# A scheduled order, later weight loads, two-bank PSUM tiles and 256-token MLP chunks in an attention, Fourier-mixing and MLP kernel

## Chip, cores and metric

One core of one Trainium2 chip. The time is device microseconds of one execution; a lower time is better. The sessions ran on different chips; in three of them the kernel before had medians of 359.4 to 360.1 us. So where two medians of different sessions lie close, the ratios, each to the kernel before on the same chip, are the safer measure.

## The reference, cut to what matters

```python
# attention: B=4 batches, H=8 heads, S=768 tokens, D=64; 8 global keys, 96 local keys
scores = scale * (q @ k^T) + bias          # bias by distance; masked outside the band
a = softmax(scores);  attn = a @ v         # -> x of shape (B, S, 512)
# mixing and MLP
X = fft(fft(x, axis=1), axis=2);  u = x + real(X)
un = (u - mean(u)) / sqrt(var(u) + 1e-6)
out = u + maximum(un @ w_ch1, 0) @ w_ch2   # 512 -> 2048 -> 512
```

Everything is float32 outside; the kernel computes its matmuls in float16 with float32 accumulation.

## The kernel before

Each batch passes through attention, mixing (the Fourier transform, as folds on DVE and matmuls `py` and `pu`), normalisation, and the MLP (`ph` is the first matmul, `pg` the second). Rows are handled by residue modulo 6, so a row tile is 128 rows with one residue. Python code emits all instructions in one order, guided by a rough clock (`ck`). Each engine then runs its own part of that order, in order; below, DVE's u adds stand behind a multiply that waits 3.27 us. The kernel uses PSUM, the memory that matmuls write, as eight banks of 512 float32 per partition. DVE and ACT read a finished bank out (an *eviction*), which makes it free for the next matmuls.

```python
XB = 5
BUFS = {"x": XB, "ph": 2, "pg": 1}               # 8 banks, each a tile of its own
def bank(tag, name, dtype=FP32):
    n = 512 if dtype == FP32 else 1024
    return ps.tile([P, n], dtype, tag=tag, name=name, bufs=BUFS[tag])
...
def u_u(b, rs):                                   # one row tile of the mixing's last matmul
        pu = bank("x", f"pu_{b}_{rs}")
        for rd, (r2, d2, mir) in enumerate(src):
            o = pu[:, rd * P:(rd + 1) * P]        # contiguous: one column class after the other
            for c in range(2):
                nc.tensor.matmul(o, yy[:, c, :], t2_sb[:, rd, ...], start=(c == 0), stop=(c == 1))
        VT(u.rearrange("p (n r) -> p r n", r=4), pu.rearrange("p (r n) -> p r n", r=4),
           XR[b][:, rs, :].rearrange("p (n r) -> p r n", r=4), op=ALU.add)
...
def u_ph(c, jb):                                  # MLP chunk of 384 tokens: three row tiles
        ph = bank("ph", f"ph_{c}_{jb}")
        for d in range(ND):
            nc.tensor.matmul(ph[:, 0:CH], w1[:, d, jb * P:(jb + 1) * P], UNT[(b, half)][:, d, :], ...)
...
def load_w():                                     # all weights on the GpSimd queue
    for a in range(4):
        nc.gpsimd.dma_start(w1[:, :, a * 512:(a + 1) * 512], ...)
    for a in range(4):
        nc.gpsimd.dma_start(w2[:, 4 * a:4 * a + 4, :], ...)
...
            if which == "A":                      # attention and mixing: one fixed list
                A[ia][3]()
                ia += 1
                if not wload and ia == 12:
                    load_w()
```

The softmax here doesn't subtract the row's maximum and nothing guards it: scores larger than these inputs give would overflow.

Of the kernel before, what the change touches and what calls it, by code (L numbers as in the profile page):

```python
# [17 lines left out]
class Clock:  # L18


    SEM = 0.12

    def __init__(self):
        self.t = {"PE": 0.0, "ACT": 0.0, "DVE": 0.0, "POOL": 0.0}
        self.tok = {}
        self.ring = {}

    def at(self, needs):
        return max([self.tok[n] for n in needs], default=0.0)
# [4 lines left out]
    def adv(self, eng, cost, after=0.0):  # L34
        end = max(self.t[eng], after + self.SEM) + cost
        self.t[eng] = end
        return end

    def slot(self, tag, bufs):
        r = self.ring.setdefault(tag, [0.0] * bufs)  # L40
        return r.pop(0)

    def give(self, tag, when):
        self.ring[tag].append(when)
        self.ring[tag].sort()

    def slot_at(self, tag, bufs, n=1):
        r = self.ring.setdefault(tag, [0.0] * bufs)
        return r[n - 1] if len(r) >= n else 1e9


def mm_us(n, k=1):
    return k * max(n / 2400.0 + 0.0025, 0.029)


@with_exitstack
def kernel(
# [20 lines left out]
    CH = S // 2  # L78
# [9 lines left out]
    dist = np.zeros((P, 512))  # L88
    dist[:, 0:256] = np.where(band, rel, np.where(kk < NG, NL, far))
    dist[:, 256:512] = np.where(band, rel, far)  # L90
    pp = np.arange(P)[:, None]
# [17 lines left out]
    gb = np.zeros((32, 2))  # L109
    for half in range(2):  # L110
        for h in range(4):
            gb[h * NG:(h + 1) * NG, half] = -slopes[4 * half + h] * NL
# [12 lines left out]
    XB = 5  # L125
    UB = 7
    BUFS = {"x": XB, "ph": 2, "pg": 1}
    ck = Clock()

    def bank(tag, name, dtype=FP32):  # L130
        n = 512 if dtype == FP32 else 1024
        return ps.tile([P, n], dtype, tag=tag, name=name, bufs=BUFS[tag])

# [3 lines left out]
    dist_sb = kon.tile([P, 512], FP16, tag="dist", name="dist")  # L137
    gb_sb = kon.tile([32, 2], FP32, tag="gb", name="gb")
# [5 lines left out]
    mhalf = kon.tile([P, NS], FP32, tag="mhalf", name="mhalf")  # L144
# [3 lines left out]
    vG = [kon.tile([32, 2, 4, 66], FP16, tag=f"vG{i}", name=f"vG{i}") for i in range(2)]  # L148


    def flex(cost_act, cost_dve, after, on_act, on_dve):

        ea = max(ck.t["ACT"], after + ck.SEM) + cost_act
        ed = max(ck.t["DVE"], after + ck.SEM) + cost_dve
        if ea <= ed:
            on_act()
            return ck.adv("ACT", cost_act, after)
        on_dve()
        return ck.adv("DVE", cost_dve, after)

    stage = {}

    def load(b, hp):
        for nm, src in (("q", q), ("k", k), ("v", v)):
            if b == 0 and nm != "v":
                if hp == 0:
                    stage[(nm, "all")] = wk.tile([P, HP, S], FP32, tag="hT", name=f"{nm}s0", bufs=2)
                t = stage[(nm, "all")][:, hp, :]
            elif b == 0 and hp >= 2:
                t = wk.tile([P, S], FP32, tag="unT", name=f"{nm}s_{b}_{hp}", bufs=2)  # L170
            else:
                t = wk.tile([P, S], FP32, tag=f"{nm}s", name=f"{nm}s_{b}_{hp}", bufs=2 if nm == "v" else 1)
            stage[(nm, b, hp)] = t
            for s in range(2):
                dst = t.rearrange("p (i h d) -> p i h d", h=2, d=Dh)[:, :, s, :]
                nc.sync.dma_start(dst, src[b, 2 * hp + s].rearrange("(i p) d -> p i d", p=P))  # L176
            base = 3.5 + 2.3 * hp if b == 0 else max(ck.t["PE"], ck.tok.get(("cast", nm, b, hp - 1), 0)) + 6
            ck.tok[("ld", nm, b, hp)] = base + {"q": -0.7, "k": 0.0, "v": 0.7}[nm]

    T16 = {}  # L180
    TT = {}

    def u_cast(b, hp, nm):
        def run():
            src = stage[(nm, b, hp)]
            after = ck.tok[("ld", nm, b, hp)]
            if nm == "v":
                dst = v16[b % 2][:, :, 2 * hp:2 * hp + 2, 0:Dh]
                src = src.rearrange("p (i h d) -> p i h d", h=2, d=Dh)
                if b == 0:  # L190
                    nc.gpsimd.tensor_copy(dst, src)  # L191
                    end = ck.adv("POOL", 1.0, after)
                else:
                    nc.gpsimd.tensor_copy(dst, src)
                    end = ck.adv("POOL", 1.0, after)
            else:
                t = wk.tile([P, S], FP16, tag=f"{nm}16", name=f"{nm}16_{b}_{hp}", bufs=2)
                T16[(nm, b, hp)] = t
                end = flex(0.83, 0.5, after,
                           lambda: nc.scalar.activation(t, src, AF.Copy),  # L200
                           lambda: nc.vector.tensor_copy(t, src))  # L201
            ck.tok[("cast", nm, b, hp)] = end
            nxt = HP * b + hp + 1
            if nm == "v" and HP <= nxt < HP * B:
                load(*divmod(nxt, HP))
        return ([("ld", nm, b, hp)], None, 0, run)

    def u_trans(b, hp, nm):
        def run():
            src = T16.pop((nm, b, hp))  # L210
            pt = bank("x", f"pt{nm}_{b}_{hp}", FP16)
            dst = wk.tile([P, S], FP16, tag=f"{nm}T", name=f"{nm}T_{b}_{hp}", bufs=3)
            TT[(nm, b, hp)] = dst
            free = ck.slot("x", XB)
            for i in range(NS):
                nc.tensor.transpose(pt[:, i * P:(i + 1) * P], src[:, i * P:(i + 1) * P], idn)
            e = ck.adv("PE", mm_us(P, NS), max(ck.at([("cast", nm, b, hp)]), free)) + 0.15
            end = flex(0.85, 0.55, e,
                       lambda: nc.scalar.activation(dst, pt[:, 0:S], AF.Copy),
                       lambda: nc.vector.tensor_copy(dst, pt[:, 0:S]))  # L220
            ck.give("x", end)
            ck.tok[(nm + "T", b, hp)] = end
            if nm == "k":
                for s in range(2):
                    c0 = 16 * (hp % 2) + 8 * s
                    nc.gpsimd.tensor_copy(kG[b % 2][64 * s:64 * s + 64, hp, c0:c0 + NG],
                                          dst[64 * s:64 * s + 64, 0:NG])
                    ck.tok[("kG", b, hp)] = ck.adv("POOL", 0.15, end)
        return ([("cast", nm, b, hp)], "x", 1, run)

    def u_score(b, hp, g):
        def run():
            qT, kT = TT[("q", b, hp)], TT[("k", b, hp)]
            n1 = 224 if g < 2 else P
            n = 256 + n1
            pa = [bank("x", f"sc_{b}_{hp}_{g}_{s}") for s in range(2)]
            free = max(ck.slot("x", XB), ck.slot("x", XB))
            for i, c0, w in ((2 * g, 0, 256), (2 * g + 1, 256, n1)):
                for s in range(2):
                    lo = 64 * s  # L240
                    nc.tensor.matmul(pa[s][:, c0:c0 + w], kT[lo:lo + 64, i * P:(i + 1) * P],  # L241
                                     qT[lo:lo + 64, i * P:i * P + w], start=True, stop=True)
            e = ck.adv("PE", 0.25, max(ck.at([("qT", b, hp), ("kT", b, hp)]), free)) + 0.15
            er = wk.tile([P, 2, 480], FP16, tag="er", name=f"er_{b}_{hp}_{g}", bufs=2)
            for s in range(2):
                nc.scalar.activation(er[:, s, 0:n], pa[s][:, 0:n], AF.Exp, 0.0, 0.125)  # L246
                end = ck.adv("ACT", 0.19 + n / 1200, e)
                ck.give("x", end)
            m0 = 0 if g == 0 else 256
            nc.vector.tensor_tensor(expst[hp][:, :, g * 512:g * 512 + n], er[:, :, 0:n],  # L250
                                    mk[:, 2 * hp:2 * hp + 2, m0:m0 + n], op=ALU.mult)
            ck.tok[("ex", b, hp, g)] = ck.adv("DVE", 0.15 + n / 960, end)
        return ([("qT", b, hp), ("kT", b, hp)], "x", 2, run)

    def u_vg(b):
        def run():
            pv = bank("x", f"pvg_{b}")
            free = ck.slot("x", XB)
            for half in range(2):
                for h in range(4):  # L260
                    c0 = half * 256 + h * 64
                    nc.tensor.matmul(pv[0:32, c0:c0 + 64], sel_sb[0:NG, h * 32:(h + 1) * 32],  # L262
                                     v16[b % 2][0:NG, 0, 4 * half + h, 0:Dh], start=True, stop=True)
# [155 lines left out]
    def u_y(b, n):  # L419
        needs = [("w", b)]  # L420

        def run():
# [24 lines left out]
            if n == len(YP) - 1:  # L447
                mirror(b, end)
# [326 lines left out]
```

## Time and profile before

| | before |
|---|---|
| time, median of 4 runs | 361.1 us (359.4 to 361.5) |
| span of the profiled run | 357.4 us |
| busy PE, DVE, ACT, POOL | 272.4, 210.5, 142.6, 51.5 us |
| last v of batch 0 cast at | 46.3 us |
| first ph at | 87.0 us |
| after the first ph: length, PE busy, PE idle | 270.4, 238.7, 31.6 us |

PE is TensorE, PEld its weight loads, DVE VectorE, ACT ScalarE, POOL GpSimd and SP SyncE. L569 is a source line; lines move by a few between kernels, so the same group has a number near it in the others. Busy time by stretches, cut at the first ph. Its columns are the stretch and its length, then busy us (and instructions) of PE, weight loads, DVE, ACT and POOL, then the mean granted clock of PE, the DMA share and GB/s. The kernel before:

```profile
0.00:87.02 87.02, 33.69 (x293) 21.97 (x294) 45.12 (x114) 25.21 (x46) 19.74 (x42) 0.96 0.79 146
87.02:357.40 270.38, 238.74 (x1808) 133.54 (x1807) 165.37 (x357) 117.43 (x236) 31.74 (x71) 0.96 0.38 90
```

The idle time of a stretch is its length less PE's busy time: 53.3 us before the first ph and 31.6 after.

### The profile page before, as it was taken

What the parts mean: (1) busy time and instruction counts of PE and PEld (TensorE: products, weight loads), DVE (VectorE), ACT (ScalarE), POOL (GpSimd) and SP (SyncE); (2) the same over time, 40 slices, a digit from 0 to 9 for tenths busy, and PEclk for the clock granted to TensorE, in tenths of its full rate; (3) what the DMA queues carried; (4) which work ended last, traced back from release to release, by engine and by line L of the source; (5) the groups of instructions that cost most, each with busy time, mean ns of one, the idle gap of its engine ahead of it and who ended that gap; (6) DMA issues with size and microseconds to landing.
All of it is one profiled execution on the core that took longest, in us unless ns stands there. A gap on an engine that the chain in (4) does not pass through costs nothing.

```text
span 357.4 us, 5463 instructions
## 1 busy us (share of the span) xinstructions
PE 272.4 (76%) x2100; PEld 155.5 (44%) x2100; DVE 210.5 (59%) x470; ACT 142.6 (40%) x282; POOL 51.5 (14%) x113
## 2 busy tenths in 40 slices
PE   0540079246899998838999989389999994799995
PEld 0320045134555554635555546255545452555542
DVE  0730049978555689796456976984567778810011
ACT  1840053012587730215778312056965220355310
POOL 1760010031121000312120003121110003100000
PEclk9999999996999999969999999879999998799999
DMA  9999990400397606101986043009900250000011
GB/s 187 217 201 196 196 244 1 172 6 1 88 207 166 132 2 193 73 29 43 213 175 132 31 124 142 29 2 202 192 33 32 88 179 0 31 0 29 31 58 60
DMA packets 87306, 36.99 MB, mean 104 GB/s; under 512 B 76016, under 2 KB 83440, under 8 KB 87280
## 3 DMA queue, kind: packets, MB, share of 16 engines
q1 hardware_dynamic: 83056, 32.45, 40.5%
q0 software_dynamic: 4224, 4.19, 6.9%
q8 instruction: 16, 0.26, 0.3%
q14 instruction: 10, 0.08, 0.1%
HBM read 31.39 MB, written 9.44 MB: 114 GB/s over the span
## 4 chain that ended last, share of the span: by engine, by line
PE 57%; DVE 22%; SPq 8%; DMA 7%; issue 2%; POOL 2%; ACT 1%; POOLq 0%; DVEq 0%
PE pg L598 21%; PE ph L569 19%; DMA vs<-in_v_dram 7%; SPq L176 7%; DVE u L495 7%; DVE st L503 5%; PE pav L324 4%; PE sc L241 3%; DVE ob L603 2%; PE py L429 2%; DVE un L523 2%; PE ptu L545 2%; PE pav L313 2%; PE pu L490 2%; PE py L432 1%
## 5 line engine op out<-in xcount | busy, mean ns | idle before, releaser
L569 PE MATMUL ph<-unT,w 128*128 128x384 f16 x512 | 97.9, 329 | 2.7 <-ACT unT L549 2.7
L598 PE MATMUL pg<-w,hT 128*128 128x512 f16 x384 | 94.3, 379 | 3.3 <-DVE ob L603 2.6
L574 ACT ACTIVATE hT<-ph 128x384 f16<-128x384 f32 x117 | 57.7, 499 | 60.5 <-PE ph L569 60.2
L569 PEld LDWEIGHTS <-w 128*128 128x128 f16 x512 | 48.2, 99 | 42.2 <-issue 10.0
L250 DVE TENSOR_TENSOR ex<-er,mk 128x960 f16<-128x960 f16 (+1 forms) x48 | 31.8, 665 | 40.4 <-ACT er L246 40.2
L598 PEld LDWEIGHTS <-hT 128*128 128x128 f16 x384 | 36.2, 98 | 40.6 <-issue 6.0
L246 ACT ACTIVATE er<-sc 128x480 f16<-128x480 f32 (+1 forms) x96 | 45.9, 556 | 8.1 <-PE sc L241 6.4
L603 DVE TENSOR_TENSOR ob<-pg,u 128x512 f32<-128x512 f32 x24 | 16.5, 688 | 40.3 <-PE pg L598 38.6
L545 PE MATMUL ptu<-ident,un 128*128 128x128 f16 x96 | 12.2, 266 | 28.6 <-DVE un L523 28.1
L495 DVE TENSOR_TENSOR u<-pu,xr 128x512 f32<-128x512 f32 x24 | 25.4, 1057 | 8.4 <-PE pu L490 8.4
L549 ACT ACTIVATE unT<-ptu 128x512 f16<-128x512 f16 x12 | 7.2, 597 | 55.8 <-PE ptu L545 55.8
L441 ACT ACTIVATE y<-py 128x512 f16<-128x512 f32 x16 | 9.2, 596 | 40.2 <-PE py L432 39.9
L545 PEld LDWEIGHTS <-un 128*128 128x128 f16 x96 | 7.9, 121 | 33.1 <-DVE un L523 33.1
L332 DVE TENSOR_TENSOR x<-pav,rc 128x256 f16<-128x256 f32 x48 | 20.4, 425 | 1.6
L241 PE MATMUL sc<-qT,kT 64*128 64x256 f16 x192 | 19.0, 290 | 2.9 <-ACT q L200 2.1
L324 PE MATMUL pav<-v,ex 128*128 128x65 f16 x352 | 20.6, 207 | 0.0
L262 PE MATMUL pvg<-v,ident 8*32 8x64 f16 x32 | 2.3, 198 | 23.2 <-POOL v L191 23.0
L324 PEld LDWEIGHTS <-ex 128*128 128x128 f16 x352 | 15.2, 105 | 8.2 <-issue 4.4
L503 DVE BATCH_NORM_STATS2 st<-u 128x6 f32<-128x512 f32 x24 | 16.7, 695 | 0.8
L523 DVE TENSOR_SCALAR un<-u,mv,rstd 128x512 f16<-128x512 f32 x24 | 13.1, 599 | 5.3 <-POOL rstd L509 5.3
L455 POOL COPY rev<-y 128x2 f16<-128x2 f16 x4 | 0.8, 192 | 99.0 <-PE py L432 99.0
L201 DVE CAST k<-ks 128x768 f16<-128x768 f32 x13 | 7.2, 556 | 12.9 <-DMA ks<-in_k_dram 12.9
(81 smaller groups left out, 309.4 us busy)
## 6 DMA issues: line engine op xcount, KB each, us to landing
qs<-in_q_dram SPq DMA_DIRECT2D x32, 192.0 KB, 3.7
ks<-in_k_dram SPq DMA_DIRECT2D x32, 192.0 KB, 4.0
vs<-in_v_dram SPq DMA_DIRECT2D x32, 192.0 KB, 4.5
out_dram<-ob SPq DMA_DIRECT2D x24, 256.0 KB, 2.0
w<-in_moe_w_ch_dram POOLq DMA_DIRECT2D x8, 512.0 KB, 15.6
xd<-x SPq DMA_DIRECT2D x4, 768.0 KB, 3.7
xr<-xd SPq DMA_DIRECT2D x4, 768.0 KB, 4.9
t<-t1m SPq DMA_DIRECT2D x1, 384.0 KB, 16.7
```

What stands on the lines that cost most here:

```text
L176: nc.sync.dma_start(dst, src[b, 2 * hp + s].rearrange("(i p) d -> p i d", p=P))
L241: nc.tensor.matmul(pa[s][:, c0:c0 + w], kT[lo:lo + 64, i * P:(i + 1) * P], qT[lo:lo + 64, i * P:i * P + w], start=True, stop=True)
L246: nc.scalar.activation(er[:, s, 0:n], pa[s][:, 0:n], AF.Exp, 0.0, 0.125)
L250: nc.vector.tensor_tensor(expst[hp][:, :, g * 512:g * 512 + n], er[:, :, 0:n], mk[:, 2 * hp:2 * hp + 2, m0:m0 + n], op=ALU.mult)
L324: nc.tensor.matmul(o, lhsT, v16[b % 2][:, i, h, 0:65], start=(j < 2 and a == 0), stop=(a == len(ops) - 1), skip_group_check=True)
L495: VT(u.rearrange("p (n r) -> p r n", r=4), pu.rearrange("p (r n) -> p r n", r=4), XR[b][:, rs, :].rearrange("p (n r) -> p r n", r=4), op=A ...
L503: nc.vector.bn_stats(st, u)
L545: nc.tensor.transpose(pt[:, c * P:(c + 1) * P], un[:, c * P:(c + 1) * P], idn)
L569: nc.tensor.matmul(ph[:, 0:CH], w1[:, d, jb * P:(jb + 1) * P], UNT[(b, half)][:, d, :], start=(d == 0), stop=(d == ND - 1))
L574: lambda: nc.scalar.activation(dst, ph[:, 0:CH], AF.Relu),
L598: nc.tensor.matmul(pg, HT[c][:, jb, t * P:(t + 1) * P], w2[:, jb, :], start=(jb == 0), stop=(jb == NJ - 1))
L603: nc.vector.tensor_tensor(ob, pg, UT[(b, rs)], op=ALU.add)
```

## The change

A list scheduler with a clock per engine, a queue of loads and priorities (mixing, then attention, then pg, then ph) decides the order of all work. Attention and mixing get two-bank PSUM tiles, so that one eviction serves two banks. MLP chunks shrink from three row tiles to two, so that an MLP can start earlier. The weight loads also move: w1 after the third v cast, w2 to batch 0's mixing. The core of the diff, of some 1,500 lines:

```diff
-    BUFS = {"x": XB, "ph": 2, "pg": 1}
+    RING = {"xx": 2, "ph": 2, "pg": 2}
+    cd = [ps.tile([P, 2, 512], FP32, tag=f"c{i}", name=f"c{i}", bufs=1) for i in range(2)]
...
     def bank(tag, name, dtype=FP32):
-        n = 512 if dtype == FP32 else 1024
-        return ps.tile([P, n], dtype, tag=tag, name=name, bufs=BUFS[tag])
+        if tag in "CD":                                  # batch 0's attention borrows both
+            return cd["CD".index(tag)]
+        if tag in turn:                                  # ph and pg: slices of one tile each
+            turn[tag] += 1
+            return cd["ph pg".index(tag) // 3][:, turn[tag] % 2, :]
+        return ps.tile([P, 2, 512 if dtype == FP32 else 1024], dtype, tag=tag, name=name, bufs=RING[tag])
...
-                o = pu[:, rd * P:(rd + 1) * P]
+                o = pu[:, a, :].rearrange("p (n r) -> p r n", r=4)[:, rd, :]
...
-            VT(u.rearrange("p (n r) -> p r n", r=4), pu.rearrange("p (r n) -> p r n", r=4),
-               XR[b][:, rs, :].rearrange("p (n r) -> p r n", r=4), op=ALU.add)
+                VT(u, pu, XR[b][:, r0:r1 + 1:r1 - r0, :], op=ALU.add)
...
-                if not wload and ia == 12:
-                    load_w()
+        for i in range(8):
+            needs = [("v", 0, 2)] if i == 0 else [("rv", 0, 0)] if i == 4 else [("wl", i - 1)]
+            pl.later([("POOL", 0.85, lambda i=i: wload(i))], needs, ...)
...
+        pl.run([(MIX, True), (ATT, True), (PG, False), (PH, False)])
```

## The prediction

> **What bounds the kernel now.** I read the busy shares of the slices first, then busy time stage by stage, then the wait list, and last the timeline of the first 90 us. TensorE (PE) is the busiest engine, 272.4 of 357.4 us, and the slices show where it is not:
>
> ```profile
> PE   0540079246899998838999989389999994799995
> ...
> DMA  9999990400397606101986043009900250000011
> ```
>
> One digit is 8.9 us. PE is at 9 through most of the second half, but nearly empty in the first five slices while the DMA is full, and it dips (8 3 8, 9 3 8, 4 7) once per batch. I cut the span by stage:
>
> ```profile
> 0.00:25.00 25.00, 9.59 (x72) 5.86 (x73) 10.52 (x30) 13.86 (x25) 14.34 (x30) 1.00 1.20 202
> 25.00:46.00 21.00, 0.00 (x0) 0.00 (x0) 1.12 (x2) 0.00 (x0) 0.00 (x0) 1.00 1.22 199
> 46.00:64.20 18.20, 14.68 (x136) 8.19 (x135) 13.39 (x41) 7.76 (x15) 1.19 (x3) 1.00 0.47 102
> 64.20:87.00 22.80, 9.41 (x84) 7.92 (x85) 20.06 (x41) 3.58 (x6) 4.20 (x9) 0.85 0.20 70
> 87.00:313.60 226.60, 199.45 (x1601) 113.43 (x1601) 160.81 (x350) 103.47 (x208) 31.74 (x71) 0.95 0.43 100
> 313.60:357.40 43.80, 39.30 (x209) 20.11 (x206) 4.58 (x7) 13.96 (x29) 0.00 (x0) 0.98 0.10 36
> ```
>
> Columns: stretch and length, then busy us of PE, weight loads, DVE, ACT, POOL, then granted clock, DMA share, GB/s. From 25 to 46 us no engine computes and the DMA moves 199 GB/s. At 64.2 batch 0's attention is complete; up to 87.0, where the first MLP matmul (ph) starts, batch 0's mixing runs on DVE (20.06 of 22.8 us) with PE mostly empty. From 87.0 on it is a PE-bound kernel: 238.75 us busy in 270.4, so 31.6 idle. The waits name the culprits:
>
> ```profile
> PE ptu L545 <- DVE un L523: 28.1, 8, 6.9
> ...
> POOL v L191 <- DMA vs<-in_v_dram: 22.0, 1, 22.0
> ...
> PE pg L598 <- DVE ob L603: 2.6, 3, 1.1
> ```
>
> The first is the per-batch dip: in the mixing PE waits up to 6.9 us for a normalised tile. About 21 of its 28.1 us lie after 87.0. The second is the hole at the start, and the timeline shows its cause:
>
> ```profile
> 20.95 9.72 SPq L176 DMA_DIRECT2D vs<-in_v_dram  x2
> ...
> 46.29 0.82 POOL L191 CAST v<-vs 128x768 f16<-128x768 f32 x1 [22.04 <-DMA vs<-in_v_dram]
> ```
>
> The last head pair's v is issued at 20.95 and usable only at 46.29, because all eight weight loads (4.19 MB as written) were queued from 16.3 us on and share the DMA with it; and the fixed order puts a step that needs every v ahead of scores and outputs that do not.
>
> [...] from 20 to 46 us the input queue got about 1.6 MB of 5.4. [...]
>
> ```profile
> 103.16 0.65 PE ph L569 x4
> ...
> 139.34 3.61 PE pg L598 x16
> ```
>
> 0.65/4 = 162 ns for 384 columns; 3.61/16 = 226 ns for 512 columns, with the last drain in it. [...] The residual add of 512 took 688 ns [...], but the strided u add 1057:
>
> ```profile
> L495 DVE TENSOR_TENSOR u<-pu,xr 128x512 f32<-128x512 f32 x24 | 25.4, 1057 | 8.4 <-PE pu L490 8.4
> ```
>
> [...] the change makes the pu output stride 4.
>
> **The change part by part.**
>
> *Start.* Only half the weights (w1, 2.1 MB) may start early, after the third v is cast; w2 waits for mixing and batch 1's loads for batch 0's round trip. The nine transfer pairs through the third v are 3.5 MB plus constants; at some 205 GB/s they land near 20 us, so w1 starts near 21. About 1.1 MB of input is then left, and w1 takes 2.1/0.134 = 16 us at the share weights had before ((5.4-1.6) MB in 26 us, about 140). I put the last v at 37 us, not 46. The new order has by then done all other scores, so cast, outputs and norm need about 5 us, not 18: attention of batch 0 ends near 42 instead of 64.2.
>
> *Mixing to first ph.* Fold of the second half 3.2, first fold_d part 1.9, second 2.1, py with its eviction 2.7, pu 1.0, [...] statistics 2 x 0.69 + 2 x 0.18 = 1.75, four small POOL steps 1.4, two normalisations on ACT 1.3, transposes 0.8, eviction 1.0, semaphores about 1: 19 us against 22.8, because it waits for one pair of row tiles instead of three. First ph near 61-62: 25 us earlier.
>
> *PE work after that.* ph goes from 512 x 384 to 768 x 256 columns: 512 x 162 = 83.0 us against 768 x 109 = 83.8. Matmul columns are otherwise equal (2100 instructions become 2360, the 256 ph and four tiny ones). So 239 us of busy time stay, perhaps 3 less from fewer cold stretches (clock 0.85 in the mixing stage).
>
> *DVE and ACT.* u adds 12 x 1.22 = 14.6 instead of 25.4; half as many reciprocals, -4; norms 24 x 0.69 = 16.5 instead of 20.4; 17 of 24 normalisations move to ACT, -9; transposed q/k copies all come to DVE, +4; folds in one piece, -5. DVE about 192 instead of 210, ACT about 137 instead of 143. Neither bounds before or after; this only shortens the dip.
>
> *Dips.* The order keeps earlier MLP chunks for the gaps. For batch 1 that fails: all three chunks of batch 0 are done before its mixing matmuls, and only the next batch's scores fill in. DVE chain there about 22 us, PE work in it 19, plus latency: 5-6 us lost. Batches 2 and 3 have ph and pg between: 1-2 each. So 21 becomes 8, gain 13.
>
> *What it adds.* I also read which instruction each wait in the built program names. The two ph banks are now slices of one tile, and so are the two pg banks, and waits are by tile: a ph unit waits for the eviction of the unit before it, in the other bank; two ph units in a row are evicted only when both are done. The ring of two is a ring of one. Working through the 53 such ph waits (eviction plus signalling 0.9 us for one, 1.4 for two, less the matmuls placed between) leaves 14 us, the 21 pg waits (0.69 add + 0.2) 8 us. The same sum for the kernel before gives 3 + 4, where the wait list shows about 5. So +15 us.
>
> *Sum.* After the first ph: 239 - 3 + (31.6 - 13 + 15) = 270, as long as before (270.4). The gain is the start's 25: 61.5 + 270 = 331 span; runs lie 3.4 above the profiled span (360.8 against 357.4), giving 335. My whole-tile sum counts each wait in full, though other waits and drain overlap (ph lasts 326 ns but is spaced 162) will swallow a third: -5. **330 us.**
>
> **Rivals.** *A: the strided pu output costs PE.* 192 matmuls; if each doubles from 56 to 107 ns, +10 us, a third of it in the dips. [...] Against: each has its own weight load of about 98 ns, which may hide it. Makes it 335-340. *B: the start stays load-bound*, since w1 alone still competes with the last v: if it lands at 44 instead of 37, 337. *C: the whole-tile waits are mostly hidden or the dips vanish entirely*: 315. *D: DVE becomes the bound*: 192 us in 330 is 58%, so no; only if its order is wrong in a mixing stage. *E: in-order stalls where the scheduler's clock and the chip disagree* (single q/k staging buffer, POOL casts behind late loads): 10-15 us, 345. *F: the early start is a mirage because the PE sum bounds*: no, 239 + 61 is well below.
>
> **Range and chances.** A, B and E each raise it by 5-15 and are partly exclusive; C lowers it by 15. So 330, 8 in 10 within 309 to 345. "Same" needs over 353.6, two of the bad rivals at full size: 4%; slower needs the plan to fail: 2%.
>
> **What would show it.** In the changed profile: last v of batch 0 cast at 34-40 us and first ph at 58-66; busy PE 230-242 after it; the u add near 1.22 us; pu per matmul near 60 ns (A wrong) or above 100 (A right); many PE waits of ph on hT evictions, 10-20 us in sum where there were none; one dip near mixing 1, next to none at 2 and 3. The prediction is wrong if the first ph comes as late as 75, or if these ph waits are under 5 us, or if a wait on a load appears after batch 0.

One term of the sum: the add of 1024 columns, 1.22 us, in the list from mixing to the first ph. With it the list came to 19.4 us, without it 18.15. The forecast used 19: first ph at 42 + 19 = 61 to 62; then 61.5 + 270 = 331 of span, + 3.4 for the time, - 5 for waits swallowed: 330 us. The term can also be had from the profile before, as an estimate: DVE's TENSOR_TENSOR took 425 ns for 256 columns (x<-pav,rc) and 688 for 512 (ob<-pg,u), so 688 + 2 x 263 = 1.21 us for 1024; in the changed kernel it took 1.218. For the doubling that rival A supposes no reason is left; 56 and 107 ns are in the profile before, but as the pu spacing at granted clocks of 1.00 and 0.50.

- 109 ns for 256 columns: the ph spacing in the changed kernel.
- 0.69 us: 695 ns of a BATCH_NORM_STATS2 and 688 of a TENSOR_TENSOR of 512 columns in the kernel before.
- 1.6 MB of 5.4: a misreading, 1.12 of 5.17 by the DMA packets.
- The "last drain": pg matmuls of the kernel before start 216 ns apart and are drawn 379 long; 15 x 216 + 379 = 3.61 us.
- "Semaphores" and "signalling": in the timeline of the changed kernel below, ACT ends at 288.37 + 1.09 = 289.46 and the ph that needs both evictions starts at 289.51. From 288.17, when the ph unit before has made way for pg, it is 0.85 us to the pg that waits for one eviction (289.02) and 1.34 to that ph, where the forecast has 0.9 and 1.4.
- 3 us less for "cold" stretches, those of a low granted clock: a guess; after the first ph the clock was 0.96 before and 0.98 after.

## The result, and the profile after

The changed kernel takes **341.2 us** (median of 4, 339.8 to 341.4) against 361.1: ratio 0.945, 95% interval 0.941 to 0.949. A ratio here is the mean time of one kernel's runs over that of the other's of the same rounds, so it is not quite the ratio of the medians.

The slices of the changed kernel; one digit is 8.5 us:

```profile
PE   0596385898989986589998999898998999989894
```

The two empty slices near the start are gone, but there are many 8s where the second half had 9s before. Busy time by stretches says the same with numbers (cut where batch 0's attention is complete and at the first ph):

```profile
0.00:37.96 37.96, 22.56 (x212) 14.69 (x212) 23.56 (x57) 20.85 (x27) 9.26 (x25) 1.00 1.12 215
37.96:60.00 22.04, 11.74 (x81) 9.07 (x82) 16.99 (x37) 4.88 (x8) 8.69 (x19) 0.98 0.98 189
60.00:339.70 279.70, 249.62 (x2068) 162.30 (x2067) 141.13 (x241) 101.77 (x151) 61.82 (x121) 0.98 0.35 89
```

The first ph starts 27 us earlier (60.0 against 87.0), yet what follows takes 279.7 us instead of 270.4: 9.3 us are given back. The timeline of the changed kernel (start, duration, engine, line, what; in brackets the idle time before and who ended it) shows the start as it was meant, and one thing that was not:

```profile
24.21 0.74 POOL L913 DMA_DIRECT2D w<-in_moe_w_ch_dram  x1
29.12 0.82 POOL L343 CAST v<-u 128x768 f16<-128x768 f32 x1 [4.17 <-DMA u<-in_v_dram]
...
132.00 1.91 PE L723 MATMUL pu<-t,zy 128*128 128x128 f16 x16 [0.69 <-ACT zy L659]
```

The last v is cast at 29.1 instead of 46.3. The pu matmuls, in a stretch at granted clock 1.00, take 1.91 us for 16; their starts lie 109 ns apart (the last is drawn 314 ns long). The kernel before had 22 in 1.39 us at that clock, about 55 ns apart. But 64 of its 192 pu matmuls ran at a granted clock of 0.50, and lay 107 ns apart there. In the groups of the changed kernel (columns: in the prediction) the u add has become one contiguous add of 1024:

```profile
L740 DVE TENSOR_TENSOR u<-pu,xr 128x1024 f32<-128x1024 f32 x12 | 14.5, 1218 | 7.3 <-PE pu L723 6.5 <-DMA vs<-in_v_dram 0.9
```

The wait list (who waited for whom: us in total, times, longest) has lost the prediction's wait of ptu for un, and has these instead; `c` is the tile of both ph banks at L814 and of both pg banks at L837:

```profile
PE c L837 <- DVE ob L848: 7.1, 11, 0.8
...
PE c L837 <- ACT hT L820: 5.1, 20, 0.3
PE c L814 <- ACT hT L820: 4.0, 9, 0.7
```

They sum to 16.2 us (ACT and DVE write hT, the evicted ph; DVE adds pg into ob). The timeline of the last stage, where nothing but MLP is left, shows one period of them (PE's matmuls, and ACT's evictions up to the second wait):

```profile
286.43 1.91 PE L814 MATMUL c<-unT,w 128*128 128x256 f16 x16
288.17 0.59 PE L837 MATMUL c<-w,hT 128*128 128x512 f16 x2
288.37 1.09 ACT L820 ACTIVATE hT<-c 128x512 f16<-128x512 f32 x2 [5.67 <-PE c L814]
289.02 0.60 PE L837 MATMUL c<-w,hT 128*128 128x512 f16 x2 [0.26 <-ACT hT L820]
289.51 1.91 PE L814 MATMUL c<-unT,w 128*128 128x256 f16 x16
```

Two ph units and one part of pg take 289.51 - 286.43 = 3.08 us, of which the profile calls 0.26 idle.

### The profile page after: what moved, and what is told of

Its sections match the earlier page's. It is cut to its first block, busy times and chain, and to the rows that moved or that the text cites. A ratio compares the mean times of both kernels' runs of the same rounds, so it can differ in the third digit from the quotient of the medians.

```text
span 339.7 us, 5828 instructions
## 1 busy us (share of the span) xinstructions
PE 283.9 (84%) x2360; PEld 186.1 (55%) x2360; DVE 181.7 (53%) x332; ACT 127.5 (38%) x185; POOL 79.8 (23%) x165
## 4 chain that ended last, share of the span: by engine, by line
PE 64%; ACT 8%; DVE 7%; SPq 7%; DMA 5%; POOL 4%; issue 4%; POOLq 0%; DVEq 0%; ACTq 0%
PE c L814 26%; PE c L837 22%; ACT hT L820 5%; SPq L320 4%; PE pav L494 3%; PE pu L723 3%; PE sc L397 2%; DMA u<-in_v_dram 2%; DVE ob L848 2%; PE pav L481 2%; SPq L309 2%; PE pt L369 2%; DMA vs<-in_v_dram 2%; PE py L643 2%; DMA xr<-xd 1%
## 5 line engine op out<-in xcount | busy, mean ns | idle before, releaser
L837 PE MATMUL c<-w,hT 128*128 128x512 f16 x384 | 98.9, 380 | 12.6 <-DVE ob L848 7.1
L814 PE MATMUL c<-unT,w 128*128 128x256 f16 x768 | 98.6, 279 | 5.1 <-ACT hT L820 4.0
L820 ACT ACTIVATE hT<-c 128x512 f16<-128x512 f32 x85 | 48.0, 596 | 120.7 <-PE c L814 113.1
L814 PEld LDWEIGHTS <-w 128*128 128x128 f16 x768 | 75.4, 100 | 26.3 <-issue 11.6
L837 PEld LDWEIGHTS <-hT 128*128 128x128 f16 x384 | 33.3, 97 | 53.5 <-ACT hT L820 15.9
L405 ACT ACTIVATE er<-sc 128x960 f16<-128x960 f32 (+1 forms) x42 | 38.0, 910 | 31.6 <-PE sc L397 30.8
L848 DVE TENSOR_TENSOR ob<-c,u 128x512 f32<-128x512 f32 x24 | 16.5, 689 | 55.1 <-PE c L837 55.0
L410 DVE TENSOR_TENSOR ex<-er,mk 128x960 f16<-128x960 f16 (+1 forms) x48 | 33.4, 700 | 21.3 <-ACT er L405 21.1
L333 POOL CAST qk<-qs 128x768 f16<-128x768 f32 x24 | 21.2, 903 | 36.5 <-PE pt L369 21.5
L692 POOL COPY ww<-zy 128x512 f16<-128x512 f16 x16 | 9.4, 613 | 61.5 <-PE py L643 43.1
L375 DVE COPY qkT<-pt 128x1536 f16<-128x1536 f16 x16 | 15.3, 954 | 13.1 <-PE pt L369 13.1
L369 PE MATMUL pt<-ident,qk 128*128 128x128 f16 x192 | 15.8, 242 | 4.5 <-DVE qk L331 2.4
L659 ACT ACTIVATE zy<-py 128x512 f16<-128x512 f32 (+1 forms) x12 | 9.6, 810 | 23.4 <-PE py L646 17.9
L768 ACT ACTIVATE un<-u,rstd 128x512 f16<-128x512 f32 x17 | 13.4, 810 | 12.3 <-POOL rstd L758 11.1
L397 PE MATMUL sc<-qkT 64*128 64x256 f16 (+2 forms) x168 | 16.0, 281 | 1.0 <-DVE unT L796 1.0
```

The source lines that it names most:

```text
L333: nc.gpsimd.tensor_copy(d, s)
L369: nc.tensor.transpose(pt[:, w, j * P:(j + 1) * P], src[:, w, j].rearrange("p h d -> p (h d)"), idn)
L375: V.tensor_copy(TT[n], pt[:, :, 0:S])
L397: nc.tensor.matmul(pa[:, s, c0:c0 + cw], TT[n][lo:lo + 64, 1, i * P:(i + 1) * P], TT[n][lo:lo + 64, 0, i * P:i * P + cw], start=True, stop ...
L405: A(er[0][:, :, 0:w], pa[:, :, 0:w], AF.Exp, 0.0, 0.125)
L410: VT(expst[hp][:, :, g * 512:g * 512 + w], er[0][:, :, 0:w], mk[:, 2 * hp:2 * hp + 2, m0:m0 + w], op=ALU.mult)
```

## The experiments

Twelve kernels ran, three timed rounds each, all with correct results. The orders of instructions called equal below are so in the traces. Ratios are against runs of the kernel before on the same chip (359.4 to 360.1 us median). First ph and the length after it are from each profiled run.

| kernel | time, us | ratio (95%) | first ph | after it |
|---|---|---|---|---|
| before | 361.1 | 1 | 87.0 | 270.4 |
| changed | 341.2 | 0.945 (0.941-0.949) | 60.0 | 279.7 |
| b_latew: before, weights late | 340.4 | 0.945 (0.942-0.949) | 67.7 | 271.5 |
| a_earlyw: changed, weights early | 361.0 | 1.002 (0.997-1.007) | 80.4 | 279.9 |
| a_sep: changed, ph and pg banks apart | 317.9 | 0.882 (0.878-0.886) | 59.7 | 257.2 |
| a_sep_ph: changed, ph banks alone apart | 324.8 | 0.904 (0.900-0.907) | 60.0 | 263.8 |
| b_slice: b_latew, ph banks as slices | 382.8 | 1.064 (1.061-1.067) | 67.5 | 313.5 |
| a_pu: changed, pu contiguous | 337.9 | 0.938 (0.934-0.942) | 59.5 | 276.7 |
| a_pu_sep: a_sep and a_pu together | 316.0 | 0.877 (0.872-0.882) | 60.8 | 254.3 |
| a_perm_sep: a_sep, u in class order | 314.8 | 0.873 (0.868-0.878) | 59.4 | 250.6 |
| a_q: changed, round trip off the SP queue | 342.0 | 0.949 (0.946-0.953) | 60.6 | 280.9 |
| a_pu_sep_q: all three | 316.8 | 0.880 (0.877-0.884) | 61.4 | 253.8 |
| a_sep_prio: a_sep, MLP first | 366.5 | 1.018 (1.014-1.023) | 59.5 | 303.6 |
| a_sep_look1: a_sep, look-ahead 1 | 329.1 | 0.915 (0.911-0.918) | 62.9 | 264.3 |

The theory was the prediction's: a gain at the start, from the weights no longer competing with inputs and from the order; and a loss after it, from waits by whole tile. The rivals were that the strided pu output is the loss, that an in-order stall is, or that the order alone makes the gain.

### Are the weights the gain? (b_latew, a_earlyw)

In the kernel before, with the same order on PE, ACT and DVE:

```diff
-                if not wload and ia == 12:
-                    load_w()
-                    wload = True
+                if ia == 16:          # after batch 0's third v cast
+                    load_w1()
+                if ia == NA0 + 9:     # as batch 0's mixing starts
+                    load_w2()
```

> The kernel before, with its old order and tiles; only the weight loads move: the four of w1 are queued after batch 0's third v is cast, the four of w2 where batch 0's mixing starts. Theory (the hole at the start is weights competing with the last inputs): last v of batch 0 cast at 29 to 36 us instead of 46.3, first ph 10 to 15 us earlier than 87.0, time 346 to 352 us against 361, so over half of the change's gain at the start comes from this alone. Rival (the fixed order is what holds the start, or the weights are now late for ph): first ph still after 83 us, time within 3 us of 361.

And the reverse, in the changed kernel, whose scheduler then places some later work differently too:

```diff
-            needs = [("v", 0, 2)] if i == 0 else [("rv", 0, 0)] if i == 4 else [("wl", i - 1)]
+            needs = [("v", 0, 1)] if i == 0 else [("wl", i - 1)]
```

> The changed kernel with its own order, but all eight weight loads queued early again, from batch 0's second v cast on, as in the kernel before. Theory (weights compete with inputs): last v of batch 0 cast at 42 to 48 us instead of 29.1, first ph at 70 to 75 instead of 60.0, time 350 to 356 against 341. Rival (the scheduled order hides late inputs): first ph before 64, time within 4 us of 341.

Moving eight loads in the old kernel gave **340.4 us**, as fast as the whole change, and better than expected. Putting them back in the changed kernel gave **361.0**, as slow as the kernel before, 5 us worse than expected. b_latew, timeline and busy time by stretches:

```profile
26.68 0.82 POOL L191 CAST v<-vs 128x768 f16<-128x768 f32 x1 [2.23 <-DMA vs<-in_v_dram]
```

```profile
67.70:339.20 271.50, 239.09 (x1808) 133.71 (x1807) 165.18 (x357) 117.33 (x236) 31.66 (x71) 0.96 0.39 92
```

a_earlyw, the same two views:

```profile
48.52 0.82 POOL L343 CAST v<-u 128x768 f16<-128x768 f32 x1 [23.85 <-DMA u<-in_v_dram]
```

```profile
80.40:360.30 279.90, 250.39 (x2068) 162.91 (x2067) 137.76 (x237) 101.58 (x152) 60.06 (x120) 0.97 0.34 85
```

The last v comes at 26.7 to 29.1 us with w1 alone behind it and at 46.3 to 48.5 with all eight loads; the first ph follows, and the length after it does not move (271.5 against 270.4; 279.9 against 279.7). So 87.0 - 67.7 = 19.3 of the 27.0 us gained at the start are the weights, and 67.7 - 60.0 = 7.7 the new order with its smaller chunks. Taken the other way round, with a_earlyw, they are 80.4 - 60.0 = 20.4 and 6.6. The early loads are not only more: they are also issued at 15.5 to 16.3 us, against 20.5 to 21.1, and no run separates their number from their time. The net gain of the change is no more than the weights; all else came out at about zero. Either the rest is worth nothing, or it is worth much and something takes it away.

### Do waits by whole tile take it away? (a_sep, a_sep_ph, b_slice)

Four single-bank tiles take the place of the two double ones, in the same four banks, once batch 0's attention has given those up. Every engine has the same instructions in the same order; only waits differ.

```diff
-    cd = [ps.tile([P, 2, 512], FP32, tag=f"c{i}", name=f"c{i}", bufs=1) for i in range(2)]
+    cdp = tc.tile_pool(name="cdp", bufs=1, space=bass.MemoryType.PSUM)
+    cdt = cdp.__enter__()
+    cd = [cdt.tile([P, 2, 512], FP32, tag=f"c{i}", name=f"c{i}", bufs=1) for i in range(2)]
+    mlp = {}
...
-            turn[tag] += 1
-            return cd["ph pg".index(tag) // 3][:, turn[tag] % 2, :]
+            if not mlp:
+                cdp.__exit__(None, None, None)
+                mlp[0] = ctx.enter_context(tc.tile_pool(name="mlp", bufs=1, space=bass.MemoryType.PSUM))
+            return mlp[0].tile([P, 512], FP32, tag=tag, name=name, bufs=2)
```

> The changed kernel with the two ph banks and the two pg banks as four tiles of their own, opened when batch 0's attention has given up the two double banks; engine orders identical, only waits differ. Theory of the prediction (waits by whole tile cost 22 us in sum, a third hidden): time 326 to 334 against 341, ph pairs in the last stage spaced about 2.7 us instead of 3.08. Rival C (these waits are mostly hidden): over 337.

**317.9 us: 23.3 less** (22.7 by the ratios), more than expected. The stage after the first ph falls from 279.7 to 257.2 us. The same place in the timeline of a_sep (PE's matmuls and the first of ACT's evictions), and its stretch after the first ph:

```profile
285.49 1.91 PE L819 MATMUL ph<-unT,w 128*128 128x256 f16 x16
286.56 0.60 ACT L825 ACTIVATE hT<-ph 128x512 f16<-128x512 f32 x1 [4.59 <-PE ph L819]
287.23 1.03 PE L842 MATMUL pg<-w,hT 128*128 128x512 f16 x4
288.10 1.91 PE L819 MATMUL ph<-unT,w 128*128 128x256 f16 x16
```

```profile
59.70:316.90 257.20, 243.93 (x2068) 164.59 (x2067) 140.09 (x241) 104.34 (x151) 64.14 (x121) 0.97 0.39 96
```

The period is 288.10 - 285.49 = 2.61 us, against 3.08, without a gap. The profile had called only 0.26 of these 0.47 us idle. The same shows in the sum: of the 22.5 us saved after the first ph, idle time gives 30.1 - 13.3 = 16.8, and **busy PE gives 249.6 - 243.9 = 5.7**, though the work is the same. The reason, as a reading of the trace: pg matmuls start 216 ns apart but are drawn 379 ns long, so the last one before a wait covers its first 0.16 us. The changed kernel has 32 gaps right after a ph or pg matmul and a_sep has 2, which makes (32 - 2) x 0.16 = 4.8 of the 5.7 us, as an estimate. So a sum of PE's waits reads low.

a_sep_ph leaves the pg banks as slices of one tile:

```diff
+            if tag == "ph":
+                return mlp[0].tile([P, 512], FP32, tag=tag, name=name, bufs=2)
+            turn[tag] += 1
+            return mlp["pg"][:, turn[tag] % 2, :]      # one double tile, as in the change
```

> The changed kernel with only the two ph banks as tiles of their own; the two pg banks stay slices of one tile. Splits the 23 us. By the prediction's sums (14 us of ph waits, 8 of pg waits) ph alone should give about 15 of the 23: 325 to 328 against 341. Rival (one of them is nearly all, since a ph wait also delays the pg behind it): below 321 if it is all ph, above 333 if pg.

324.8 us: ph's share is 16.4 us and pg's 6.9 by the medians, 15 and 8 by the ratios. The prediction's sums were 14 and 8. The ph share is not visible as waits of ph alone (4.0 us in the list). Where two ph units follow each other, both are evicted only when both are done: in the timeline above ACT writes hT first at 288.37, after the second unit, and in a_sep at 286.56, during it. So it is the pg part that reads the first one's hT that waits. The wait list of a_sep_ph agrees: PE's 5.1 and 4.0 us of waits for hT shrink to 0.5, and the 7.1 for ob stay (7.2).

The opposite test puts this one thing into the old order (b_latew):

```diff
+    phs = ps.tile([P, 2, 512], FP32, tag="phs", name="phs", bufs=1)
     def bank(tag, name, dtype=FP32):
+        if tag == "ph":
+            turn[0] += 1
+            return phs[:, turn[0] % 2, :]
```

> The kernel before with late weights, and one thing taken from the change: its two ph banks become the two halves of one tile. Order of all work unchanged. Theory (waits go by tile, so a ring of two slices is a ring of one): the same sum that gave 14 us of ph waits for the changed kernel gives about 54 us more here (121 waits, up to 0.9 us each, since this order puts more ph units back to back): 375 to 395 against 340.4. Rival (the cost seen in the changed kernel is peculiar to its order, not to slices): under 350.

382.8 against 340.4, so **42.4 us slower**, within the expected range. Its wait list names the line, again with fewer us than are lost:

```profile
PE phs L575 <- ACT hT L580: 30.0, 44, 1.4
```

So the cost belongs to the slices, not to the new order. Why the new order suffers less is not tested. By count of the traces fewer of its ph units follow another directly, 32 of 96 against 49 of 128.

### What does the strided pu output cost? (a_pu, a_pu_sep, a_perm_sep)

```diff
-                o = pu[:, a, :].rearrange("p (n r) -> p r n", r=4)[:, rd, :]
+                o = pu[:, a, rd * P:(rd + 1) * P]
...
-                VT(u, pu, XR[b][:, r0:r1 + 1:r1 - r0, :], op=ALU.add)
+                for a, r in enumerate((r0, r1)):
+                    VT(u[:, a].rearrange("p (n r) -> p r n", r=4), pu[:, a].rearrange("p (r n) -> p r n", r=4),
+                       XR[b][:, r, :].rearrange("p (n r) -> p r n", r=4), op=ALU.add)
```

> The changed kernel with the pu output contiguous again (each of the four column classes in its own 128 columns), and the u add done as two strided adds of 512, as in the kernel before; order of all other instructions the same. Theory (stride-4 PSUM writes slow the matmul): pu spaced 55 ns instead of 109, busy PE 10 us less; the adds cost 2 x 1.06 instead of 1.22 us per pair; about two thirds of the 10 us is saved, time 333 to 337 against 341. Rival (the pu time lies in dips and the slower adds eat it): within 2 us of 341.

337.9 us, 3.3 less (2.6 by the ratios, whose intervals just overlap); expected were 4 to 8. At granted clock 1.00 the spacing is 55 ns again, and the adds take 2 x 1.08 us. PE is busy 277.4 us instead of 283.9: 6.5 less, not the 10 expected.

> The changed kernel with both edits: ph and pg banks as four tiles, and the pu output contiguous with two strided adds. With the banks apart PE is busy nearly without a gap after 60 us but for batch 1's mixing, so a saving in PE now counts in full. Theory (strided pu costs 10 us of PE, of which the three later batches' 7.7 us lie on the bounded path): 309 to 312 against 317.9 with the banks alone, busy PE about 268. Rival (the slower adds or something else fills the place, as the 3.3 us of the pu edit alone suggest): 314 to 318.

316.0 us against 317.9: 1.9 less (ratios 0.877 and 0.882, with overlapping intervals). The theory was wrong twice: PE's work fell by 6.8 us (278.3 to 271.5), not 10, and the time by less. Two stretches show it, the first with batch 1's mixing, the second with those of batches 2 and 3. In a_sep:

```profile
120.00:150.00 30.00, 21.17 (x165) 15.49 (x165) 20.94 (x36) 11.76 (x15) 15.95 (x31) 0.83 0.49 115
150.00:280.00 130.00, 130.00 (x1160) 89.32 (x1159) 80.65 (x142) 58.22 (x85) 24.13 (x54) 1.00 0.20 62
```

and in a_pu_sep:

```profile
120.00:150.00 30.00, 19.78 (x163) 14.32 (x161) 23.52 (x40) 11.45 (x14) 16.30 (x32) 0.72 0.49 115
150.00:280.00 130.00, 127.86 (x1180) 85.95 (x1177) 85.21 (x149) 59.52 (x87) 23.88 (x54) 1.00 0.20 62
```

In batch 1's mixing PE idles anyway (8.8 us of 30 in a_sep, 10.2 in a_pu_sep), and pu itself gains little there, because the granted clock differs. Six pu matmuls, first of a_sep, then of a_pu_sep:

```profile
131.96 0.86 PE L728 MATMUL pu<-t,zy 128*128 128x128 f16 x6
```

```profile
130.89 0.84 PE L728 MATMUL pu<-t,zy 128*128 128x128 f16 x6
```

The strided ones ran at a granted clock of 1.00 (131.57 to 133.5), 109 ns apart; the contiguous ones at 0.50 (130.5 to 132.4), 107 apart. So all pu matmuls together took 22.4 us in a_sep and 15.8 in a_pu_sep, where 192 x (109 - 55) would be 10.4 less. Whether the edit itself lowers the clock is not shown. In batches 2 and 3, at clock 1.00, their time does fall, from 11.1 to 6.2 us. There a_sep has no idle time, and a_pu_sep gets 20 more instructions done in the same 130 us but now idles for 2.1, while DVE is 4.6 us busier with its slower adds. The first ph comes 1.1 us later (60.8 against 59.7); the slower adds alone don't explain that, since a_pu, which has them too, starts it at 59.5. So some 6.5 us of PE work (243.9 - 237.4 after the first ph) became 2.9 us there (257.2 - 254.3), and 1.9 us of time.

a_perm_sep takes both strides away where they hurt. It keeps u in the order of the column classes, loads the rows of w1 in that order, and reads u strided in the last add only:

```diff
-                VT(u, pu, XR[b][:, r0:r1 + 1:r1 - r0, :], op=ALU.add)
+                for a, r in enumerate((r0, r1)):
+                    VT(u[:, a].rearrange("p (r n) -> p r n", r=4), pu[:, a].rearrange("p (r n) -> p r n", r=4),
+                       XR[b][:, r, :].rearrange("p (n r) -> p r n", r=4), op=ALU.add)
...
-                                    moe_w_ch1[:, a * 512:(a + 1) * 512].rearrange("(c p) f -> p c f", p=P))
+                                    moe_w_ch1[:, a * 512:(a + 1) * 512].rearrange("(p c) f -> p c f", c=ND))
...
-                VT(cell[0], pg, UT[c][:, t, :], op=ALU.add)
+                VT(cell[0].rearrange("p (n r) -> p n r", r=4), pg.rearrange("p (n r) -> p n r", r=4),
+                   UT[c][:, t, :].rearrange("p (r n) -> p n r", r=4), op=ALU.add)
```

> The changed kernel with the banks apart, pu contiguous and u kept in the order of its four column classes, with the rows of w1 loaded in that same order; the column order is put right where the last add reads u. So neither PE's PSUM write nor u's write is strided; the last add reads u strided. Theory (a strided write is what slowed the u add to 1.06 us): u adds 0.7 us per 512, the mixing stage shorter, 312 to 315 against 316.0. Rival (the strided fp16 read of xr is as slow, or the strided read moves 0.37 us to each of the 24 last adds): u add or last add 1.06 us, time within 1.5 us of 316.0.

Its groups:

```profile
L855 DVE TENSOR_TENSOR ob<-pg,u 128x512 f32<-128x512 f32 x24 | 25.0, 1044 | 37.4 <-PE pg L844 37.4
...
L746 DVE TENSOR_TENSOR u<-pu,xr 128x512 f32<-128x512 f32 x24 | 15.1, 681 | 4.2 <-PE pu L728 4.2
```

Theory and rival each held in part. The u add fell from 1080 to 681 ns, so its strided write (16 bytes from one float32 to the next) was the slow operand. The strided float16 read of xr (8 bytes apart) shows no cost: the last add took 688 ns without any stride. The last add, which now reads float32 512 bytes apart, rose from 688 to 1044 ns, where the wait for it has room. At 314.8 us this is **the fastest kernel here**, 3.2 us below a_sep by the ratios (their intervals just touch) and 12.7% below the kernel before. It is within the noise of a_pu_sep (ratios 0.873 and 0.877, intervals 0.868 to 0.878 and 0.872 to 0.882).

### Does an in-order stall cost 5 us at batch 1's mixing? (a_q, a_pu_sep_q)

```diff
-                nc.sync.dma_start(XD[b][:, c].rearrange("(j p) d -> p j d", p=P), X[b][:, :, c])
+                nc.scalar.dma_start(XD[b][:, c].rearrange("(j p) d -> p j d", p=P), X[b][:, :, c])
...
-            nc.sync.dma_start(XR[b][:, 0:3], rows[:, 0:3])
-            nc.sync.dma_start(XR[b][:, 3:6], rows[:, 3:6])
+            nc.scalar.dma_start(XR[b][:, 0:3], rows[:, 0:3])
+            nc.scalar.dma_start(XR[b][:, 3:6], rows[:, 3:6])
```

> The changed kernel with the transposing round trip of x (two writes, two reads per batch) issued from ACT instead of the SP queue, where its read stood behind loads that wait for POOL's casts. Theory (rival E of the prediction: an in-order stall of about 5 us at batch 1's mixing): 335 to 338 against 341. Rival (another wait, the pu chain or the adds, ends at the same time, or ACT's issue time costs as much): 340 to 343.

> All three edits at once: banks apart, pu contiguous, round trip off the SP queue. Theory: 2 to 4 us below the kernel with the first two, about 307. Rival: no difference to it, within 1.5 us, because with the banks apart the read already arrives in time for batch 1's adds.

342.0 and 316.8 us: no gain from either. The read of xr is issued 2.2 us earlier in a_q (128.38 against 130.57), but the u adds start at 137.48 instead of 136.61. What stands ahead of them in the changed kernel is in DVE's timeline:

```profile
135.32 1.36 DVE L410 TENSOR_TENSOR ex<-er,mk 128x960 f16<-128x960 f16 x1 [3.27 <-ACT er L405]
136.61 2.34 DVE L740 TENSOR_TENSOR u<-pu,xr 128x1024 f32<-128x1024 f32 x2
```

The scheduler put a mask multiply of batch 2's scores ahead of batch 1's adds on DVE. It waited 3.27 us for an exponential, which waited for scores that PE ran behind the pu unit (a pu of 1.9 us, where the scheduler's clock has 0.9). So there is an in-order stall, but it is on DVE, not on the SP queue; a_q has it too, with 3.59 us. That is a reading of the trace. No run took that stall away; in a_pu, whose pu unit takes 1.05 us, it is 2.11 us, as the reading would have it.

### What do the priorities and the look-ahead do? (a_sep_prio, a_sep_look1)

```diff
-        pl.run([(MIX, True), (ATT, True), (PG, False), (PH, False)])
+        pl.run([(PG, False), (PH, False), (MIX, True), (ATT, True)])
```

> The changed kernel with the banks apart, and the scheduler's priorities turned round: MLP streams before mixing and attention where both could start. Theory (the priorities keep MLP work for the mixing stages): with MLP first, that work is used up and PE idles in mixing again as it did before, 5 to 15 us slower than 317.9. Rival (PE-bound whatever the order): within 3 us.

366.5 us, **48.6 slower** than a_sep, three times the upper end of what was expected; the direction held. Of a_sep_prio, the slices and two stretches of mixing:

```profile
PE   1588296999997627699999917789999918699995
```

```profile
108.00:148.00 40.00, 25.24 (x235) 18.41 (x232) 29.64 (x48) 10.35 (x13) 16.32 (x23) 0.66 0.54 126
...
190.00:240.00 50.00, 35.32 (x338) 24.86 (x337) 34.17 (x59) 16.43 (x22) 15.19 (x29) 0.86 0.21 59
```

The dips are back in every batch, and deeper than before the change: 14.8 us of 40 and 14.7 of 50 without work, at a granted clock down to 0.66. MLP work that goes first is used up by the time that the mixing needs something beside it, and the next batch's attention is late as well.

```diff
-    LOOK = 10
+    LOOK = 1
```

> The changed kernel with the banks apart, with the scheduler's look-ahead within a stream cut from 10 units to 1, so that mixing and attention keep their written order. Theory (look-ahead lets batch 0's scores pass a step that waits for v, and mixing steps pass each other): first ph later by 3 to 6 us, time 321 to 326 against 317.9. Rival (the written order already suits; the gain is from interleaving streams alone): within 2 us.

329.1 us, 11.2 slower; 3 to 8 were expected. The first ph comes 3.2 us later (62.9), as expected; the other 7.1 us are lost after it (264.3 against 257.2), which was not expected.

## Why the prediction was right or wrong

The direction and the range held: 341.2 us lies inside 309 to 345, but 11 above 330. The terms of the sum in its own form, with each measured one from the runs above:

| term, us | predicted | measured | from |
|---|---|---|---|
| first ph | 61.5 | 60.0 | changed |
| PE work after it, pu contiguous | 236 | 237.4 | a_pu_sep |
| strided pu | 0 | 6.5 | a_sep less a_pu_sep: 243.9 - 237.4 |
| idle without whole-tile waits | 31.6 - 13 - 7 = 11.6 | 13.3 | a_sep: 257.2 - 243.9 |
| whole-tile waits | 22 - 5 = 17 | 22.5 | changed less a_sep: 279.7 - 257.2 |
| span to time | 3.4 | 1.5 | 341.2 - 339.7 |
| sum | 329.5 | 341.2 | |

- **Start: the sum was right by luck, by errors that cancelled.** The last v came at 29.1, not 37. The failed term is "About 1.1 MB of input is then left", which was to share the DMA with w1. By the DMA packets of the trace 0.68 MB were left when w1 was issued at 21.1 us, and w1 moved its first packet only at 23.4, when 0.19 MB were left. (The share was misread as well: from 20 to 46 us the inputs of the kernel before got 1.12 MB of 5.17, not 1.6 of 5.4.) But attention then took 8.8 us more (37.96), not 5, and the way from there to the first ph took 22.0, not 19. That the weights make the hole is shown by b_latew and a_earlyw. What the prediction didn't see is that they are 19 to 20 of the 27 us, which the old kernel could have had by itself.
- **PE work: right.** 237.4 against 236, once pu is contiguous. In the changed kernel itself it is 249.6, outside the 230 to 242 that the prediction named: 6.5 from pu and 5.7 of waits drawn as busy time.
- **Strided pu: the failed step is "Against: each has its own weight load of about 98 ns, which may hide it".** It hid nothing: 109 ns apart, against 55 at the same clock. Rival A was right on that factor of two and too high on the rest: PE's work fell by 6.5 to 6.8 us when it was undone, largely because part of the contiguous pu ran at half the clock, and the time by 1.9 to 3.3 us. The rest lay in dips or was paid for by slower adds.
- **Dips: right in sum.** Of the 8 us given, 5 to 6 were for batch 1 and 1 to 2 for each later one. In a_sep batch 1 has 8.8 (in 30 us), and from 150 to 280 us PE has no idle time at all. Turning the priorities round cost 48.6 us.
- **Whole-tile waits: the mechanism was right; the failed step is "will swallow a third: -5".** The sum that counted each wait in full (14 + 8 = 22) was right within some 1.3 us of the measured 22.5 to 23.3. Nothing was swallowed. The reason given, that a ph lasts 326 ns but is spaced 162, works the other way: the drawn length hides waits from the reader, not from the clock.
- **The sign to look for was half wrong.** The prediction wanted 10 to 20 us of ph waiting for hT. That line has 4.0, and the prediction called itself wrong if it was under 5; the mechanism held all the same. Most of the cost shows as pg waiting (5.1 and 7.1) and as busy time (5.7).
- **Rival B fell:** the last v was no later than 29.1. **Rival C** fell: the waits were not hidden, though the later dips did vanish. **Rivals D and F fell:** DVE was busy 181.7 us of 340. **Rival E** was right that there is an in-order stall at batch 1, of 3.27 us where it gave 10 to 15. In the form tested, the SP queue, it fell: moving that transfer gained nothing.
- **Span to time:** the 3.4 set a median against the span of one run. That run itself took 359.15 us, 1.75 above its span of 357.4.

Where did the gain of so large a change go? b_latew to a_sep is 340.4 to 317.9: the order, its chunks and the rest of the change are worth 22.5 us on top of the weights. The two double tiles for ph and pg took 23.3 us, so the sum was the weights alone. The strided pu took another 2 to 3.

## What to carry to other kernels

When tiles are merged, ask what else the merge ties together: two halves of a ring in one tile are a ring of one, and a_sep got 23 us back without moving an instruction. Split a large change into its small independent parts before judging it; here moving eight loads gave as much as the whole rewrite, and hid that the rest was worth as much again. Check a wait list against the period of a repeated pattern: PE's list showed 16 of the 23 us.
